# Splitting float64 weights: exponents shifted by ScalarE's factor of 2^-112, sign bits made on GpSimd, one VectorE pass fewer

## The chip, the cores and the metric

The kernel runs on one core of one Trainium2 chip. The metric is the time of one execution in microseconds of the device (us), and lower is better. The engines are TensorE (PE in the profile; its weight loads are PEld), VectorE (DVE), ScalarE (ACT), GpSimd (POOL) and SyncE (SP, which issues most of the transfers). Each engine takes its instructions in order from a queue of its own, and engines wait for each other through semaphores. "L193" is line 193 of the kernel before.

## The reference

Local attention with 32 global tokens for 8 batches of 8 heads, then a two-layer network over the 4608 resulting rows. The part that matters here:

```python
def _moe_ref(x, w_in, w_out):
    h = x @ w_in                                                # x: 4608 x 512, w_in: 512 x 2048
    g = np.where(h > 0.0, h, np.exp(np.minimum(h, 0.0)) - 1.0)  # ELU
    return (g @ w_out).astype(np.float32)                       # w_out: 2048 x 512
```

x is the attention's output: for every local row a softmax over 32 global keys and the local keys within 32 positions, and for every global row a softmax over all keys. The weights of the network come as float64.

## The kernel before

**Two streams.** One generator, `attention()`, issues the attention of batch after batch in tiles of 128 queries (scores, exponential, sum, normalising, transposing, product with the values). Another, `ffn_stream()`, issues the network's matrix products block by block (256 rows of x at a time). A main loop interleaves both: up to yield 66 of the attention it runs alone (`lead`), and then a table (`PACE`) says how many steps of the network belong to each step of the attention. A `tick()` in the loop runs work that was put off by `defer(n, ...)` for n ticks. This gives the program order; a list scheduler then moves independent instructions past each other in each engine's queue, by its own costs. `keep_in_program_order` keeps it from moving the instruction it wraps.

**Weights.** TensorE multiplies float16 pairs: each weight is split into a high and a low float16 part after scaling by a power of two. The float64 weights are loaded as pairs of 32-bit words (`raw`, two buffers) and turned into float32 by bit operations. Sixteen units do this, eight for w_in and eight for w_out, each 128 partitions by 1024 weights. `load_weights()` takes one unit after another; `fetch` loads the next unit's words, and `unit` defers its steps:

- s0: ScalarE writes the absolute value of the high words, read as float32, into the work tile `cu` (L188); GpSimd clamps it to the range that float32 can express after the shift (L189).
- s1a: VectorE shifts the clamped word left by 3 and clears its sign and top exponent bit (L193).
- s1b: VectorE ORs in the sign and the top exponent bit, masked out of the high word (L196).
- s1c: VectorE ORs in the top three bits of the low word (L200). `cu` is now the weight in float32.
- s1d: ScalarE takes absolute values again, with their sum over the row (L204), whose output goes over the low words; `raw` is free afterwards.
- s2 to s4: a maximum over partitions (TensorE and VectorE, L141, L142), a power of two from it, the high part on ScalarE (L213) and the low part on VectorE (L216).

In the lead the steps s0 to s1d lie one tick apart, later two. The steps of the network wait for the groups of units that they need: pair 0 (group a), pair 1 (b), pairs 2 and 3 (c), pairs 4 to 7 (d), and once all are there, the later blocks use all eight at once (f) with a scheme of seven products.

**What else GpSimd does.** It normalises the attention's probabilities (L793, four per tile; L731 and L732 for the global rows) and makes small tables of factors `xs` for the network (L584 to L588), without which ScalarE cannot read the first layer's result out of TensorE's banks (L333) or scale the second layer's input (L349).

**What else VectorE does in that stretch.** The attention's masked scores with their maxima (L780), sums and reciprocals (L790, L791), the copy of the transposed probabilities (L811), maxima of x (L868), the ELU's last step (L342) and its low part (L345), the adding of partial results (L455), and the low part of x (L571).

Of the kernel before, what the change touches and what calls it, by code (L numbers as in the profile page):

```python
# [10 lines left out]
F32 = mybir.dt.float32  # L11
F32R = mybir.dt.float32r
I32 = mybir.dt.int32
AF = mybir.ActivationFunctionType
ALU = mybir.AluOpType
# [35 lines left out]
SEVEN = (((2, "B11"), (3, "B22")), ((0, "B11+B22"), (4, "B21-B11")), ((5, "B11+B12"), (1, "B22-B12")), ((6, "B21+B22"),))  # L51


FMIN = struct.unpack("f", struct.pack("I", 0x38000000))[0]
FMAX = struct.unpack("f", struct.pack("I", 0x47efe000))[0]
LOW = (127 - 40) << 23
TOP = (2 * 127 + 14) << 23

# [2 lines left out]
def attn_ffn(ctx: ExitStack, tc: tile.TileContext, qT, qgT, kT, vT, vgT, vpT, w_in, w_out, mask, out):  # L61
    nc = tc.nc
    scale = 1.0 / math.sqrt(D)
# [21 lines left out]
    def defer(n, fn):  # L85
        if n == 0:
            return fn()
        later.setdefault(now[0] + n, []).append(fn)
# [39 lines left out]
    def power(dst, src):  # L128

        dst = dst.bitcast(I32)  # L130
        nc.vector.tensor_scalar(dst, src.bitcast(I32), 0x7f800000, None, ALU.bitwise_and)
        nc.vector.tensor_scalar_max(dst, dst, LOW)

    def inverse(dst, src):

        nc.vector.tensor_scalar(dst.bitcast(I32), src.bitcast(I32), TOP, -1.0, ALU.subtract, ALU.mult)

    def all_max(dst, src):

        tp = ps_a.tile([P, 512], F32, name="pa")  # L140
        tc.keep_in_program_order(nc.tensor.transpose(tp[:, 0:P], src.to_broadcast([P, P]), ident))  # L141
        nc.vector.tensor_reduce(out=dst, in_=tp[:, 0:P], op=ALU.max, axis=AX.X)  # L142
# [34 lines left out]
    def unit(m, p, raw):  # L177
        f = slice(2 * p * P, 2 * (p + 1) * P)
        shape = [P, NC, 2 * P] if m == 0 else [P, 2, DM]
        parts = [w[:, :, f] for w in win] if m == 0 else [w[:, 2 * p:2 * p + 2, :] for w in wout]  # L180
        pw = (pww if m == 0 else pwo)[:, p:p + 1]
        u = ffn.tile(shape, F32, name="cu", bufs=3)
        mx = ffn.tile([P, 4], F32, name="cm", bufs=4)
        high, low = raw[..., 1], raw[..., 0]
        ui = u.bitcast(I32)

        def s0():
            nc.scalar.activation(u, high.bitcast(F32), AF.Abs)  # L188
            nc.gpsimd.tensor_scalar(u, u, FMAX, FMIN, ALU.min, ALU.max)  # L189

        def s1a():
            tc.keep_in_program_order(
                nc.vector.tensor_scalar(ui, ui, 3, 0x3ffffff8, ALU.logical_shift_left, ALU.bitwise_and))  # L193

        def s1b():
            nc.vector.scalar_tensor_tensor(out=ui, in0=high, scalar=-0x40000000, in1=ui,  # L196
                                           op0=ALU.bitwise_and, op1=ALU.bitwise_or)

        def s1c():
            nc.vector.scalar_tensor_tensor(out=ui, in0=low, scalar=29, in1=ui,  # L200
                                           op0=ALU.logical_shift_right, op1=ALU.bitwise_or)

        def s1d():
            nc.scalar.activation(low.bitcast(F32), u, AF.Abs, accum_out=mx[:, m:m + 1])  # L204

        def s2():
            if m == 0:
                all_max(mx[:, 1:2], mx[:, 0:1])

        def s3():  # L210
            power(pw, mx[:, 1:2])
            inverse(mx[:, 3:4], pw)
            nc.scalar.activation(parts[0], u, AF.Copy, scale=mx[:, 3:4])  # L213

        def s4():
            nc.vector.scalar_tensor_tensor(out=parts[1].rearrange("p a b -> p (a b)") if m else parts[1],  # L216
                                           in0=u.rearrange("p a b -> p (a b)") if m else u, scalar=mx[:, 3:4],
                                           in1=parts[0].rearrange("p a b -> p (a b)") if m else parts[0],
                                           op0=ALU.mult, op1=ALU.subtract)

        d = 1 if lead[0] else 2
        lag = 7 if m else 16
        for i, fn in ((1, s0), (1 + d, s1a), (1 + 2 * d, s1b), (1 + 3 * d, s1c), (1 + 4 * d, s1d),
                      (1 + lag, s2), (2 + lag, s3), (3 + lag, s4)):
            defer(i, fn)
# [758 lines left out]
    f = ffn_stream()  # L984
# [89 lines left out]
```

## Time and profile before

| | |
|---|---|
| time, median of 3 runs | 949.64 us (948.83 to 953.76) |
| the profiled execution | 954.72 us |
| its span, first to last instruction | 952.9 us |
| granted clock of TensorE, mean | 0.977 |
| instructions | 23830 |

The profile is of one execution. Busy times are sums over instructions; "idle before" is the idle time of the engine just ahead of a group of instructions, with what ended it. A row of the timeline gives the start in us from the span's start, the duration in us, the engine, the line, the operation, the tiles written and read, and in brackets how long the engine had been idle and who ended that. A wait row names the waiting instruction, the one it waited for, the total in us, how many times, and the longest. The mean over the span says little here: the start, where weights are made and the attention runs ahead, and the long rest, where TensorE is nearly always busy, have different limits.

### The profile page before, as it was taken

Reading aid. Unit: us, or ns where it says so; the run is one execution under the profiler, and the core shown is the slowest. Engines: PE = TensorE matmul, PEld = TensorE weight load, DVE = VectorE, ACT = ScalarE, POOL = GpSimd, SP = SyncE. Lnnn points to the kernel's source line nnn. Section 1 sums busy time; section 2 is a strip of 40 time slices with the busy share of each in tenths; the row PEclk is TensorE's granted clock in tenths of the full one; section 3 lists DMA queues with packets and bytes.
Section 4 is the critical chain, followed back from the end, with each engine's and each line's share of the span. In section 5 each row is a group of like instructions: output and inputs, shape, how many; then the busy total and the mean of one; then the engine's idle time right before and its main releaser. Section 6 shows DMA issues by size and latency. Waiting matters only on the chain.

```text
span 952.9 us, 23830 instructions
## 1 busy us (share of the span) xinstructions
PE 908.5 (95%) x9216; PEld 727.8 (76%) x9216; DVE 728.1 (76%) x2025; ACT 670.1 (70%) x1584; POOL 271.1 (28%) x483
## 2 busy tenths in 40 slices
PE   6889887899999999999999999999999999999997
PEld 3567564566666788888888888888888888888886
DVE  4988988889967777768776877687777777676566
ACT  5888996776656767757677767677767767666564
POOL 4655481461522322122121212221332312100000
PEclk8779999899999999999999999999999999999999
DMA  6855876331342023101330123102310101000000
GB/s 262 299 179 180 282 224 191 124 123 57 115 157 90 23 100 103 47 26 46 105 121 26 46 78 125 47 27 79 122 49 25 46 23 35 2 23 23 1 24 23
DMA packets 41769, 87.64 MB, mean 92 GB/s; under 512 B 7736, under 2 KB 8888, under 8 KB 41656
## 3 DMA queue, kind: packets, MB, share of 16 engines
q1 hardware_dynamic: 41368, 85.85, 26.6%
q8 instruction: 73, 1.20, 0.5%
q14 instruction: 40, 0.33, 0.1%
q10 hardware_dynamic: 288, 0.26, 0.1%
HBM read 70.89 MB, written 15.20 MB: 90 GB/s over the span
## 4 chain that ended last, share of the span: by engine, by line
PE 67%; DVE 14%; ACT 9%; POOL 3%; issue 3%; DMA 3%; SPq 0%; DVEq 0%; ACTq 0%; POOLq 0%
PE pa L324 25%; PE acc L482 12%; PE h L482 9%; PE acc L447 4%; PE pa L822 3%; PE h L324 3%; PE pa L769 3%; PE pa L809 2%; ACT p L786 2%; DMA raw<-w_out 2%; PE pa L889 2%; DVE gl L345 1%; POOL p L793 1%; DVE cu L196 1%; DVE cu L200 1%
## 5 line engine op out<-in xcount | busy, mean ns | idle before, releaser
L324 PEld LDWEIGHTS <-winh 128*128 128x128 f16 x2160 | 209.4, 98 | 39.2 <-issue 8.4
L793 POOL TENSOR_SCALAR p<-p,sm 128x128 f32<-128x128 f32 x256 | 147.8, 593 | 303.2 <-DVE sm L791 165.0
L324 PE MATMUL pa<-xh,winh 128*128 128x256 f16 x824 | 224.9, 273 | 0.1
L324 PE MATMUL pa<-xl,winh 128*128 128x256 f16 x824 | 224.6, 273 | 0.0
L324 PE MATMUL pa<-xh,winl 128*128 128x256 f16 x824 | 224.6, 273 | 0.0
L361 ACT ACTIVATE gh<-gx,xs 128x896 f16<-128x896 f32 x103 | 107.3, 1042 | 123.1 <-DVE gx L358 123.0
L345 DVE SCALAR_TENSOR_TENSOR gl<-gx,xs,gh 128x896 f16<-128x896 f32 x103 | 119.4, 1159 | 59.9 <-ACT gh L361 59.0
L482 PEld LDWEIGHTS <-gh 128*128 128x128 f16 x1456 | 139.5, 98 | 24.0 <-issue 7.4
L786 ACT ACTIVATE p<-p,m 128x160 f32<-128x160 f32 x256 | 106.7, 421 | 41.6 <-DVE m L780 41.4
L324 PEld LDWEIGHTS <-winl 128*128 128x128 f16 x1080 | 106.1, 98 | 14.3 <-issue 1.2
L333 ACT ACTIVATE g<-pa,xs 128x512 f32<-128x512 f32 x103 | 70.3, 682 | 24.4 <-PE pa L324 23.8
L482 PE MATMUL acc<-wouth,gh 128*128 128x256 f16 x312 | 85.2, 273 | 0.0
L482 PE MATMUL acc<-woutl,gh 128*128 128x256 f16 x312 | 85.1, 273 | 0.0
L335 ACT ACTIVATE g<-g 128x512 f32<-128x512 f32 x135 | 85.0, 630 | 0.1
L482 PE MATMUL acc<-wouth,gl 128*128 128x256 f16 x312 | 85.0, 273 | 0.0
L482 PEld LDWEIGHTS <-gl 128*128 128x128 f16 x728 | 71.2, 98 | 9.2 <-DVE gl L345 1.0
L482 PE MATMUL h<-raw,gh 128*128 128x256 f16 x416 | 75.0, 273 | 0.0
L324 PE MATMUL h<-xh,winh 128*128 128x256 f16 x256 | 71.1, 279 | 1.5 <-ACT hs L334 0.9
L324 PE MATMUL h<-xl,winh 128*128 128x256 f16 x256 | 71.0, 278 | 0.7 <-DVE xl L571 0.7
L324 PE MATMUL h<-xh,winl 128*128 128x256 f16 x256 | 71.0, 278 | 0.0
L780 DVE CUSTOM_DVE_ANT_0 p<-pa,msk 128x160 f32<-128x160 f32 x228 | 61.5, 318 | 4.8 <-PE pa L769 4.7
L342 DVE SCALAR_TENSOR_TENSOR gx<-g,hs 128x512 f32<-128x512 f32 x51 | 35.9, 704 | 36.0 <-ACT g L335 35.6
(236 smaller groups left out, 2016.9 us busy)
## 6 DMA issues: line engine op xcount, KB each, us to landing
k<-kT SPq DMA_DIRECT2D x32, 640.0 KB, 5.1
v<-vT SPq DMA_DIRECT2D x64, 256.0 KB, 2.8
q<-qT SPq DMA_DIRECT2D x32, 256.0 KB, 5.6
raw<-w_in SPq DMA_DIRECT2D x8, 1024.0 KB, 5.9
raw<-w_out SPq DMA_DIRECT2D x8, 1024.0 KB, 6.8
out<-o SPq DMA_DIRECT2D x32, 256.0 KB, 2.3
od<-o SPq DMA_DIRECT2D x24, 256.0 KB, 3.1
o<-od SPq DMA_DIRECT2D x24, 256.0 KB, 2.8
```

Source lines behind the costliest of these rows:

```text
L324: nc.tensor.matmul(h[:, j, :], wt[:, c, f], xt[:, c, :], start=k == 0, stop=k == 11)
L333: nc.scalar.activation(g, hf, AF.Relu, scale=sc[:, p:p + 1])
L335: nc.scalar.activation(g, g, AF.Exp, scale=-1.0)
L342: nc.vector.scalar_tensor_tensor(out=out, in0=ins[0], scalar=-1.0, in1=ins[1], op0=ALU.add, op1=ALU.max)
L345: nc.vector.scalar_tensor_tensor(out=dst, in0=src, scalar=sg, in1=hi, op0=ALU.mult, op1=ALU.subtract)
L361: nc.scalar.activation(gh, gx, AF.Copy, scale=sg)
L447: nc.tensor.matmul(acc[t], gt[:, s], wt[:, f, :], start=p == first and j == 0 and k == 0, stop=p == last and j == 1 and k == 2)
L482: nc.tensor.matmul(cols, gt, w, start=p == 0 and k == 0, stop=last and k == len(todo) - 1, skip_group_check=True)
L769: nc.tensor.matmul(sp[r][half * HQ:(half + 1) * HQ, j * KW:(j + 1) * KW], q[rows, qs], k[rows, t, half, :], start=True, stop=True)
L780: nc.vector.tensor_tensor_reduce(out=p, in0=sp[r][:, j * KW:(j + 1) * KW], in1=msk[:, mi, :], op0=ALU.add, op1=ALU.min, scale=-scale, scal ...
L786: nc.scalar.activation(ps[i], ps[i], AF.Exp, bias=m[:, i:i + 1], scale=-1.0, accum_out=s[:, 0, i:i + 1])
L793: nc.gpsimd.tensor_scalar(ps[i][:, 0:P], ps[i][:, 0:P], s[:, 1, i:i + 1], 1.0, ALU.mult, ALU.mult)
```

## The change

The exponent of a float64 has eleven bits and that of a float32 eight. Read as a float32, the high word of a float64 holds the top eight bits of its exponent; the old way clamps, shifts left by three and clears the two top bits of the result, to put sign and top exponent bit back from the high word. The new way multiplies by 2^-112 on ScalarE, in the instruction that takes the absolute value. That moves the exponent so far down that after the clamp (whose limits move by the same factor) the three bits that are shifted out are zero, and nothing has to be cleared. The sign bit alone is made by GpSimd, in place over the high words: (high < 0) x -2^31, written as an integer. VectorE then does the shift and the OR of the sign in one pass (L196), and the OR of the low word as before (L200). The numbers that come out are the same.

```diff
-FMIN = struct.unpack("f", struct.pack("I", 0x38000000))[0]
-FMAX = struct.unpack("f", struct.pack("I", 0x47efe000))[0]
+FMIN = 2.0 ** -126
+FMAX = struct.unpack("f", struct.pack("I", 0x0fefe000))[0]
...
         def s0():
-            nc.scalar.activation(u, high.bitcast(F32), AF.Abs)
+            nc.scalar.activation(u, high.bitcast(F32), AF.Abs, scale=2.0 ** -112)
             nc.gpsimd.tensor_scalar(u, u, FMAX, FMIN, ALU.min, ALU.max)

         def s1a():
+            nc.gpsimd.tensor_scalar(high, high.bitcast(F32), 0.0, -2.0 ** 31, ALU.is_lt, ALU.mult)
+
+        def s1b():
             tc.keep_in_program_order(
-                nc.vector.tensor_scalar(ui, ui, 3, 0x3ffffff8, ALU.logical_shift_left, ALU.bitwise_and))
-
-        def s1b():
-            nc.vector.scalar_tensor_tensor(out=ui, in0=high, scalar=-0x40000000, in1=ui,
-                                           op0=ALU.bitwise_and, op1=ALU.bitwise_or)
+                nc.vector.scalar_tensor_tensor(out=ui, in0=ui, scalar=3, in1=high,
+                                               op0=ALU.logical_shift_left, op1=ALU.bitwise_or))
```

The new GpSimd pass stands at line 192 of the changed kernel; the other lines keep their numbers. Since the scheduler places instructions by its costs, the queues change in more than these rows. They differ in the first tenth only: the last row that differs lies, by the trace of before, near 261 us, and behind it every engine's order is the same in both kernels. Three places follow. In them `cu` and `raw` are the tiles of a weight unit, `p_93` to `p_95` three tiles of probabilities, `ptw` and `ptg` the transposed ones, `pz` the probabilities of global keys, `sm` their sums, `xs` factors for the network.

GpSimd's queue at the start, from the first tile's normalising on, before:

```order
L793 TENSOR_SCALAR p_94<-p_94,sm 128x128 x3
L189 TENSOR_SCALAR cu<-cu 128x1024
L793 TENSOR_SCALAR p_94<-p_94,sm 128x128
L189 TENSOR_SCALAR cu<-cu 128x1024
L793 TENSOR_SCALAR p_95<-p_95,sm 128x128 x4
L793 TENSOR_SCALAR p_93<-p_93,sm 128x128 x4
```

and now:

```order
L793 TENSOR_SCALAR p_94<-p_94,sm 128x128 x3
L189 TENSOR_SCALAR cu<-cu 128x1024
L192 TENSOR_SCALAR raw<-raw 128x1024
L793 TENSOR_SCALAR p_94<-p_94,sm 128x128
L793 TENSOR_SCALAR p_95<-p_95,sm 128x128 x4
L189 TENSOR_SCALAR cu<-cu 128x1024
L192 TENSOR_SCALAR raw<-raw 128x1024
L793 TENSOR_SCALAR p_93<-p_93,sm 128x128 x4
```

The first sign pass stands ahead of the first tile's last normalising, and the second unit's clamp has moved behind the second tile's four, with its sign pass after it.

VectorE's queue at the same time, behind the first tile's `pz`, before:

```order
L193 TENSOR_SCALAR cu<-cu 128x1024
L811 COPY ptw_81<-pa 128x2x4x64
L196 SCALAR_TENSOR_TENSOR cu<-raw,cu 128x1024
L790 TENSOR_SCALAR sm<-sm 128x4
L780 ISA p_94,m<-pa,msk 128x160
L780 ISA m 128x1
L200 SCALAR_TENSOR_TENSOR cu<-raw,cu 128x1024
L193 TENSOR_SCALAR cu<-cu 128x1024
L791 RECIPROCAL sm<-sm 128x4
L753 TENSOR_REDUCE ptg_84<-pa 128x32
L196 SCALAR_TENSOR_TENSOR cu<-raw,cu 128x1024
```

and now:

```order
L790 TENSOR_SCALAR sm<-sm 128x4
L791 RECIPROCAL sm<-sm 128x4
L196 SCALAR_TENSOR_TENSOR cu<-cu,raw 128x1024
L795 TENSOR_TENSOR pz<-p_95,sm 128x128
L200 SCALAR_TENSOR_TENSOR cu<-raw,cu 128x1024
L811 COPY ptw_81<-pa 128x2x4x64
L790 TENSOR_SCALAR sm<-sm 128x4
L780 ISA p_94,m<-pa,msk 128x160
L780 ISA m 128x1
L196 SCALAR_TENSOR_TENSOR cu<-cu,raw 128x1024
L753 TENSOR_REDUCE ptg_84<-pa 128x32
L200 SCALAR_TENSOR_TENSOR cu<-raw,cu 128x1024
```

The second tile's sum and reciprocal have moved ahead of the first unit, the copy L811 behind it, and the reduction L753 now follows the second unit's L196 instead of its L193.

GpSimd's queue later, where the factors of group a and then c are made (by the trace of before, from 105.7 us), before:

```order
L793 TENSOR_SCALAR p_93<-p_93,sm 128x128 x4
L189 TENSOR_SCALAR cu<-cu 128x1024
L793 TENSOR_SCALAR p_94<-p_94,sm 128x128 x4
L112 MEMSET ptw_83 64x416
L584 TENSOR_SCALAR xs<-isc,xm 128x1
L585 TENSOR_SCALAR xs<-isc,xm 128x1
L588 TENSOR_SCALAR xs<-wm_a,xm 128x1
L587 TENSOR_SCALAR xs<-t_a,xm 128x1
```

and now:

```order
L793 TENSOR_SCALAR p_93<-p_93,sm 128x128 x4
L189 TENSOR_SCALAR cu<-cu 128x1024
L793 TENSOR_SCALAR p_94<-p_94,sm 128x128 x4
L192 TENSOR_SCALAR raw<-raw 128x1024
L584 TENSOR_SCALAR xs<-isc,xm 128x1
L585 TENSOR_SCALAR xs<-isc,xm 128x1
L587 TENSOR_SCALAR xs<-t_a,xm 128x1
L588 TENSOR_SCALAR xs<-wm_a,xm 128x1
```

A sign pass stands between the normalising and the factors, and the clearing of `ptw` has moved behind them.

## The prediction

> **What bounds the kernel now.** I read the totals first, then the stretches of the span, then the waits and the chain of the stretch that the change touches. The totals from the page, and three stretches with the busy time of each engine (the first number after the stretch is its length):
>
> ```profile
> PE 908.5 (95%) x9216; PEld 727.8 (76%) x9216; DVE 728.1 (76%) x2025; ACT 670.1 (70%) x1584; POOL 271.1 (28%) x483
> ```
> ```profile
> core 0: us, PE busy (x) PEld busy (x) DVE busy (x) ACT busy (x) POOL busy (x), PEclk, DMA share, GB/s
> 0.00:12.00 12.00, 9.06 (x82) 4.39 (x82) 3.51 (x23) 3.23 (x11) 2.69 (x12) 1.00 0.83 306
> 12.00:204.00 192.00, 163.08 (x1460) 110.00 (x1461) 162.92 (x505) 157.85 (x404) 105.71 (x184) 0.89 0.60 203
> 204.00:900.00 696.00, 689.80 (x7253) 572.14 (x7252) 527.76 (x1430) 480.22 (x1126) 162.16 (x287) 1.00 0.19 63
> ```
>
> From 204 to 900 us TensorE is busy for 689.80 of 696.00 us: it is the bound there, and nothing that VectorE does can shorten it. From 12 to 204 us TensorE is idle for 192.00 - 163.08 = 28.9 us. All sixteen weight units lie in this stretch, and so does every instruction of the change. Here VectorE is busy 162.92 of 192 us (85%), ScalarE 82%, GpSimd 55%. No engine is full: they hand work to each other. Whatever time is won or lost before 204 us reaches the end, since the stretch behind it is TensorE's fixed work.
>
> ```profile
> by line: DMA raw<-w_out 8.3%; issue 7.1%; POOL p L793 6.2%; DVE cu L196 6.1%; DVE cu L200 5.7%; ACT p L786 5.6%; ACT raw L204 2.7%; DVE gl L345 2.7%; DVE p L780 2.7%; DVE winl L216 2.6%; ACT gh L349 2.3%; POOL cu L189 2.3%; ACT cu L188 2.3%
> ```
> ```profile
> DVE cu L193 <- POOL cu L189: 9.4, 7, 2.9
> ...
> PE pa L809 <- POOL p L793: 4.5, 3, 3.9
> PE acc L447 <- DVE o L455: 4.2, 3, 2.2
> PE h L853 <- DVE ptg L753: 3.0, 1, 3.0
> ```
>
> The first is the chain of waits between 12 and 204 us by line; the second, the waits of the same stretch (who waited for whom: us in total, times, longest). The chain is spread over all engines; the two long VectorE passes of a unit (L196, L200) hold 11.8% of it, the pass that goes (L193) is below the lines shown. GpSimd's normalising (L793) and clamping (L189) are on it too. VectorE's largest wait is that of the removed pass itself, for GpSimd's clamp.
>
> **What goes.** Sixteen clearing passes. Their group, and two rows of VectorE's timeline:
>
> ```profile
> L193 DVE TENSOR_SCALAR cu<-cu 128x1024 int32<-128x1024 int32 x16 | 11.0, 689 | 9.4 <-POOL cu L189 9.4
> ```
> ```profile
> 78.33 0.69 DVE L193 TENSOR_SCALAR cu<-cu 128x1024 int32<-128x1024 int32 x1
> 78.94 0.68 DVE L811 COPY ptw<-pa 128x512 f32<-128x512 f32 x1
> ```
>
> A pass lasts 0.69 us, but the next instruction starts 0.61 us behind it, so 16 x 0.61 = **9.8 us** of VectorE's time come free.
>
> **What only changes form.** ScalarE's absolute value gets a factor: it had the same instruction without one, 1140 ns, and L213 with a per-partition factor on the same shape takes 1148, so I cost it at 0. VectorE's L196 now shifts and ORs instead of ANDing and ORing:
>
> ```profile
> L196 DVE SCALAR_TENSOR_TENSOR cu<-raw,cu x16: 1189/1218/1374, 18.8 to 186.2; 128x1024 int32<-128x1024 int32 x16
> L200 DVE SCALAR_TENSOR_TENSOR cu<-raw,cu x16: 1208/1218/2061, 20.3 to 187.5; 128x1024 int32<-128x1024 int32 x16
> ```
> ```profile
> L188 ACT ACTIVATE cu<-raw 128x1024 f32<-128x1024 f32 x16 | 18.2, 1140 | 6.3 <-DMA raw<-w_out 6.3
> L213 ACT ACTIVATE wouth<-cu,cm 128x1024 f16<-128x1024 f32 x8 | 9.2, 1148 | 0.5 <-DVE cm L136 0.5
> ```
>
> L200 is a shift and an OR already, over the same pair of tiles, at the same median of 1218 ns: 0 again.
>
> **What is added.** Sixteen GpSimd passes over the high words (a comparison and a product, every second word, float in and integer out). The trace has no such pass. The nearest row is L189, the same length with a minimum and a maximum, 1.04 us. From afar, L793 takes 372 ns for 128 elements; at that rate 1024 elements would take 3.0 us. The one comparison on GpSimd, an affine select, takes 0.29 us for 128, less than L793. I take **1.04 us**, since the length is what L189 shares, and keep 3.0 as the upper end.
>
> ```profile
> L189 POOL TENSOR_SCALAR cu<-cu x16: 1039/1039/1272, 15.6 to 181.3; 128x1024 f32<-128x1024 f32 x16
> L793 POOL TENSOR_SCALAR p<-p,sm x256: 362/372/5552, 14.5 to 796.5; 128x128 f32<-128x128 f32 x128
> ```
> ```profile
> 1.51 0.29 POOL masks.py:199 TENSOR_SCALAR_AFFINE_SELECT ident<-ident 128x128 f32<-128x128 f32 x1
> ```
>
> GpSimd has 192.00 - 105.71 = 86.3 us idle here, so 16.6 more would fit. But GpSimd and VectorE hold each other up. Rows of both timelines, and the usual medians of two of these groups:
>
> ```profile
> 66.79 2.14 DVE L571 SCALAR_TENSOR_TENSOR xl<-xr,xm,xh 128x1024 f16<-128x1024 f32 x1 [1.52 <-ACT xh L568]
> 94.73 2.06 DVE L200 SCALAR_TENSOR_TENSOR cu<-raw,cu 128x1024 int32<-128x1024 int32 x1
> 111.25 1.03 DVE L795 TENSOR_TENSOR pz<-p,sm 128x128 f32<-128x128 f32 x1
> ```
> ```profile
> 66.82 1.04 POOL L189 TENSOR_SCALAR cu<-cu 128x1024 f32<-128x1024 f32 x1
> 94.44 1.27 POOL L189 TENSOR_SCALAR cu<-cu 128x1024 f32<-128x1024 f32 x1 [6.03 <-ACT cu L188]
> 111.09 1.04 POOL L189 TENSOR_SCALAR cu<-cu 128x1024 f32<-128x1024 f32 x1 [3.47 <-DVE sm L791]
> 137.98 4.24 POOL L584 TENSOR_SCALAR xs<-isc,xm 128x2 f32<-128x2 f32 x1 [3.06 <-ACT o L458]
> 142.20 0.26 POOL L585 TENSOR_SCALAR xs<-isc,xm 128x2 f32<-128x2 f32 x1
> ```
> ```profile
> L571 DVE SCALAR_TENSOR_TENSOR xl<-xr,xm,xh x16: 1275/1286/2141, 66.8 to 831.9; 128x1024 f16<-128x1024 f32 x16
> L795 DVE TENSOR_TENSOR pz<-p,sm x64: 274/291/1032, 13.5 to 793.7; 128x128 f32<-128x128 f32 x64
> ```
>
> Three VectorE instructions that read two tiles of SBUF start beside a clamp and last 2.14 - 1.29 = 0.85, 2.06 - 1.22 = 0.84 and 1.03 - 0.29 = 0.74 us longer. The other way round, a two-element GpSimd operation takes 4.24 us where VectorE runs such instructions back to back, and 0.26 right behind. So a GpSimd pass is not free for VectorE even where VectorE does not need its result. What a clamp costs VectorE today: the 9.4 us of waiting, less the first and longest wait of 2.9 (VectorE had nothing else then), and the three stretches of 2.4: 8.9 us over 16, or 0.56 each. The sign pass has the same length and also stands ahead of an instruction that needs it (L196), so 16 x 0.56 = **+8.9 us**. Bounds: 0 if every pass falls into VectorE's one-tile work, and 16 x 0.56 x 3.0/1.04 = 26 us at the long price.
>
> By the Trainium skill ("SBUF — State Buffer", Who interferes with whom), a VectorE instruction with two SBUF inputs and a GpSimd instruction that reads SBUF exclude each other for the whole instruction; the trace's 2.14 against 1.29 us agrees. Read strictly, each sign pass would cost its whole length, and the sum would be that of the second rival below.
>
> **Two places where order matters.** At the start, GpSimd and VectorE run:
>
> ```profile
> 15.65 1.04 POOL L189 TENSOR_SCALAR cu<-cu 128x1024 f32<-128x1024 f32 x1
> ```
> ```profile
> 22.11 0.26 DVE L753 TENSOR_REDUCE ptg<-pa 128x32 f32<-128x128 f32 x1
> ```
>
> L753 releases TensorE's L853, which waits 3.0 us for it (above). It now stands behind the second unit's L196, and that behind these GpSimd steps: clamp from 15.65, sign (17.7), one normalising (18.1), four (19.6), clamp and sign (21.7). L196 takes 1.22, so L753 starts at 22.9 instead of 22.1 if nothing collides: +0.8. With GpSimd disturbed as it is today (eight normalisings take 5.1 us at 22.28 instead of 8 x 0.37 = 3.0) it is 1.0 more. I take **+1.0**. Part of the rest is made up, since VectorE gets the second tile's sums (L790, L791) earlier.
>
> ```profile
> 22.28 5.09 POOL L793 TENSOR_SCALAR p<-p,sm 128x128 f32<-128x128 f32 x8 [3.50 <-DVE sm L791]
> ```
> ```profile
> 131.82 0.72 ACT L349 ACTIVATE gh<-g,xs 128x512 f16<-128x512 f32 x1 [0.87 <-POOL xs L587]
> 190.10 0.69 ACT L333 ACTIVATE g<-h,xs 128x512 f32<-128x512 f32 x1 [2.77 <-POOL xs L587]
> ```
>
> Twice ScalarE waits for the factors xs from GpSimd, whose queue holds clamps ahead of them; a sign pass now stands there too. That is 0 to 2 x 1.04 us; I take the middle, **+1.0**. Behind ScalarE's waiting instruction queue the exponentials and the evictions of TensorE's banks.
>
> **Sum:** -9.8 + 8.9 + 1.0 + 1.0 = +1.1 us on the profiled execution, which took 954.72 us (span 952.9 and 1.8 around it). That run is 5.1 us above the median of 949.64; the terms are the same for both, so the forecast is 949.64 + 1.1 = **950.7 us**: no change that can be measured. About 0.5%, 4.75 us, is what a measurement of this kernel can tell from none.
>
> **Rivals.**
> Faster, 0.22: GpSimd's 86.3 idle us take the sign passes. In the 7 units where VectorE waited for the clamp it waits a little longer and wins nothing; in the other 9 it keeps 0.61 us, 5.5 us in all: 944.1. For it speaks that L196 stands later in VectorE's queue than L193 stood; against it, the 7 waits.
> Slower, 0.18: VectorE's two-tile instructions and GpSimd's passes exclude each other, and each sign pass takes its full 1.04 us from VectorE: 16 x (1.04 - 0.61) = +6.9, or 956.5. It decides once a pass costs VectorE more than 0.78 us (16 x 0.17 + 2.0 = 4.75). For it speak the three stretches of 0.74 to 0.85; against it, that only three of the sixteen clamps did as much.
> Slower still, 0.10: the comparison, the stride of two words and the integer output make the pass twice as long, 2.1 us. It then takes 2 x 0.56 from VectorE: 16 x (1.12 - 0.61) = +8.2, and the order terms double, +4.0: 961.8. The trace has no strided GpSimd row that decides. The Trainium skill ("GPSIMD Engine Reference", Performance pitfalls for Q7 kernels) puts the dearer reads at steps of over 8 bytes; here the step is 8, and no run here shows it yet.
>
> **Numbers.** Forecast 0.50, the rest as above. The forecast's own range is 946 to 955. Faster than by 0.5%: 0.22; within: 0.50; slower: 0.18 + 0.10 = 0.28. The range of 943 to 959 takes in the first two rivals and leaves out most of the third and the far ends (939.8 if the passes cost nothing, some 970 at 3.0 us each).
>
> **What would show it.** In the profile after: the sign pass's group at about 1.04 us x16; no row of the clearing pass; VectorE 11 us less busy in total unless two-tile instructions are stretched, GpSimd some 17 us more; VectorE waiting for the sign pass at L196 in about as many places as it waited for the clamp, for about as long or longer; L753 at about 23 us; the stretch behind 204 us unchanged. I am wrong if the sign pass lasts 2 us or more, if TensorE's idle time before 204 us moves by over 5 us, or if VectorE's waits for GpSimd vanish.

## The result, and the profile after

| | time, us | runs |
|---|---|---|
| before | 949.8 (948.83 to 953.76) | 4 |
| after | 984.9 (984.37 to 985.24) | 4 |

The ratio is 1.0359 [1.0332, 1.0386]: 3.6% slower, some 35 us, where no change was forecast. Here and below, an execution over 1.5% longer than the fastest of its kernel, at a lower granted clock, is left out. Each ratio is taken against executions of the kernel before in the same comparison, whose median moves between 949 and 952 us; so kernels of different tables compare by their ratios. The profiled execution of the changed kernel took 984.68 us; its span is 982.6 us at a mean granted clock of 0.966, against 952.9 us and 0.977 before, so the two spans are 29.7 us apart.

The group of the new pass, by its line (shortest, median and longest of the sixteen in ns, then the first and last start in us):

```profile
L192 POOL TENSOR_SCALAR raw<-raw x16: 3712/3817/4618, 16.7 to 209.3; 128x1024 int32<-128x1024 f32 x16
```

It lasts 3.8 us, not 1.04, and more than the 3.0 that the prediction kept as the upper end. The totals of the page, and the same stretches of the span as before:

```profile
PE 913.2 (93%) x9216; PEld 729.2 (74%) x9216; DVE 726.9 (74%) x2009; ACT 672.7 (68%) x1584; POOL 323.4 (33%) x499
```
```profile
core 0: us, PE busy (x) PEld busy (x) DVE busy (x) ACT busy (x) POOL busy (x), PEclk, DMA share, GB/s
0.00:12.00 12.00, 9.09 (x82) 4.33 (x82) 3.56 (x23) 3.29 (x12) 2.69 (x12) 1.00 0.83 311
12.00:204.00 192.00, 144.28 (x1286) 96.17 (x1287) 139.35 (x422) 137.34 (x353) 141.15 (x165) 0.83 0.57 190
204.00:900.00 696.00, 683.54 (x7155) 560.77 (x7153) 530.67 (x1459) 484.00 (x1147) 179.08 (x321) 1.00 0.19 66
```

From 12 to 204 us TensorE is now idle for 192.00 - 144.28 = 47.7 us (28.9 before), and from 204 to 900 us for 12.5 (6.2 before), since the last weight units have slipped past 204 us. That is 25.1 us more of idle time. The remaining 4.7 us are TensorE's busy time: 913.2 against 908.5 us for the same 9216 products, at a lower granted clock (0.83 against 0.89 in the first of these stretches). GpSimd is 52.3 us busier and VectorE only 1.2 us less busy, though 11.0 us of clearing passes are gone.

The waits between 12 and 204 us (who waited for whom, total, times, longest), and the chain of waits of that stretch by line:

```profile
DVE cu L196 <- POOL raw L192: 23.5, 8, 5.2
...
ACT raw L204 <- DVE cu L200: 20.6, 7, 6.8
...
PE pa L809 <- POOL p L793: 12.5, 5, 4.0
...
PE h L853 <- DVE ptg L753: 8.4, 1, 8.4
```
```profile
by line: POOL raw L192 20.1%; issue 9.6%; DVE cu L196 5.1%; ACT p L786 4.6%; POOL cu L189 4.4%; PE h L324 4.2%; DVE cu L200 4.0%; POOL p L793 3.9%; PE acc L447 3.7%; ACT raw L204 3.0%; PE h L822 2.7%; PE pa L769 2.5%; DMA raw<-w_in 2.3%; AC
```

VectorE waits 23.5 us for the sign passes (it waited 9.4 for the clamp), ScalarE waits behind VectorE, and TensorE waits 12.5 instead of 4.5 us for GpSimd's normalising and 8.4 instead of 3.0 for L753. The sign pass alone is a fifth of the chain. Both timelines of the start show how (start, duration, and in brackets the idle time ahead and who ended it); GpSimd first:

```profile
15.59 1.04 POOL L189 TENSOR_SCALAR cu<-cu 128x1024 f32<-128x1024 f32 x1
16.72 3.75 POOL L192 TENSOR_SCALAR raw<-raw 128x1024 int32<-128x1024 f32 x1
20.44 3.92 POOL L793 TENSOR_SCALAR p<-p,sm 128x128 f32<-128x128 f32 x5
24.44 1.04 POOL L189 TENSOR_SCALAR cu<-cu 128x1024 f32<-128x1024 f32 x1
25.56 3.71 POOL L192 TENSOR_SCALAR raw<-raw 128x1024 int32<-128x1024 f32 x1
```
```profile
20.50 1.22 DVE L196 SCALAR_TENSOR_TENSOR cu<-cu,raw 128x1024 int32<-128x1024 int32 x1 [3.63 <-POOL raw L192]
...
29.31 1.23 DVE L196 SCALAR_TENSOR_TENSOR cu<-cu,raw 128x1024 int32<-128x1024 int32 x1 [5.24 <-POOL raw L192]
30.45 0.28 DVE L753 TENSOR_REDUCE ptg<-pa 128x32 f32<-128x128 f32 x1
```

The two passes delay the first two units, and L753, which needs neither of them, stands behind the second unit's L196 in VectorE's queue. It starts at 30.45 us instead of 22.11.

### The profile page after: what moved, and what is told of

The parts are those of the page before. It is cut to its first block, busy times and chain, and to the rows that moved or that the text cites. A ratio compares the mean times of both kernels' runs of the same rounds, so it can differ in the third digit from the quotient of the medians.

```text
span 982.6 us, 23838 instructions
## 1 busy us (share of the span) xinstructions
PE 913.2 (93%) x9216; PEld 729.2 (74%) x9216; DVE 726.9 (74%) x2009; ACT 672.7 (68%) x1584; POOL 323.4 (33%) x499
## 4 chain that ended last, share of the span: by engine, by line
PE 65%; DVE 12%; ACT 8%; POOL 8%; issue 4%; DMA 2%; SPq 0%; DVEq 0%; POOLq 0%; ACTq 0%
PE pa L324 24%; PE acc L482 12%; PE h L482 9%; POOL raw L192 4%; PE pa L822 4%; PE acc L447 3%; PE pa L769 3%; PE h L324 3%; PE pa L809 2%; ACT p L786 2%; PE pa L889 2%; POOL p L793 1%; DVE gl L345 1%; DVE cu L196 1%; DVE cu L275 1%
## 5 line engine op out<-in xcount | busy, mean ns | idle before, releaser
L793 POOL TENSOR_SCALAR p<-p,sm 128x128 f32<-128x128 f32 x256 | 143.0, 575 | 304.5 <-DVE sm L791 191.2
L345 DVE SCALAR_TENSOR_TENSOR gl<-gx,xs,gh 128x896 f16<-128x896 f32 x103 | 119.7, 1162 | 60.3 <-ACT gh L361 59.3
L333 ACT ACTIVATE g<-pa,xs 128x512 f32<-128x512 f32 x103 | 70.6, 685 | 23.5 <-PE pa L324 22.9
L192 POOL TENSOR_SCALAR raw<-raw 128x1024 int32<-128x1024 f32 x16 | 63.0, 3936 | 1.0
```

The lines of the kernel that those rows point to most:

```text
L192: nc.gpsimd.tensor_scalar(high, high.bitcast(F32), 0.0, -2.0 ** 31, ALU.is_lt, ALU.mult)
L333: nc.scalar.activation(g, hf, AF.Relu, scale=sc[:, p:p + 1])
L345: nc.vector.scalar_tensor_tensor(out=dst, in0=src, scalar=sg, in1=hi, op0=ALU.mult, op1=ALU.subtract)
L793: nc.gpsimd.tensor_scalar(ps[i][:, 0:P], ps[i][:, 0:P], s[:, 1, i:i + 1], 1.0, ALU.mult, ALU.mult)
```

## The experiments

Edits are against the changed kernel where nothing else is said. Where a kernel leaves something out of the computation, its expectation says so.

### What makes the pass long

Three things set the new pass apart from the clamp: it compares, it steps over two words, and it writes integers. Three variants of its one line, all with the order of the changed kernel on every engine:

```diff
-            nc.gpsimd.tensor_scalar(high, high.bitcast(F32), 0.0, -2.0 ** 31, ALU.is_lt, ALU.mult)
+            nc.gpsimd.tensor_scalar(high.bitcast(F32), high.bitcast(F32), 0.0, 0.0, ALU.is_lt, ALU.mult)   # float output
...
+            nc.gpsimd.tensor_scalar(high, high.bitcast(F32), 0.0, 0.0, ALU.min, ALU.max)                   # min and max
...
+            nc.gpsimd.tensor_scalar(high.bitcast(F32), high.bitcast(F32), 0.0, 1.0, ALU.mult, ALU.mult)    # times zero
```

The third keeps the whole computation: a negative number times 0.0 is -0.0, which has the sign bit alone.

> The changed kernel with one thing altered: the sign pass on GpSimd still compares with 0 and still steps over two words, but its output is float32 zeros in place of int32 sign words. The signs of the weights are left out of the computation. Three theories on why the pass lasts 3.8 us in place of the forecast 1.04. Integer output (the conversion is dear): the pass falls to about 1.0 to 1.3 us, and the time to about 951 us. Comparison: it stays at 3.7 to 3.9 us, and the time at about 985 us. Step of 8 bytes: stays at 3.7 to 3.9 us, about 985 us.

> The changed kernel with the comparison and the multiplication of the sign pass replaced by a minimum and a maximum with 0; the int32 output and the step of two words stay. The signs of the weights are left out of the computation. Integer output: the pass stays at 3.7 to 3.9 us and the time at about 985 us. Comparison: the pass falls to 1.0 to 1.3 us, the time to about 951 us. Step of 8 bytes: stays at 3.8 us, about 985 us.

> The changed kernel with the sign word made by a multiplication of the float32 by 0.0 (and by 1.0), whose -0.0 has the sign bit alone: no comparison, no integer output, the same step of two words, the whole computation kept. Integer output or comparison, alone or both: the pass falls to 1.0 to 1.3 us, and by the forecast's sum the time is 950.7 us (943 to 959), no change within 0.5% of the kernel before. Step of 8 bytes: the pass stays at 3.8 us, and the time at about 985 us. If the pass falls and the time does not, the loss is not in the pass's length, but in the wait for GpSimd as such.

The pass by its line, in this order:

```profile
L192 POOL TENSOR_SCALAR raw<-raw x16: 3712/3848/4665, 17.1 to 207.7; 128x1024 f32<-128x1024 f32 x16
```
```profile
L192 POOL TENSOR_SCALAR raw<-raw x16: 1083/1130/1952, 16.9 to 184.8; 128x1024 int32<-128x1024 f32 x16
```
```profile
L192 POOL TENSOR_SCALAR raw<-raw x16: 1087/1140/1951, 17.2 to 186.3; 128x1024 f32<-128x1024 f32 x16
```

| | the pass, median | time, us |
|---|---|---|
| after (comparison, integer output) | 3.82 us | 984.9 |
| float output | 3.85 us | 983.24, one execution |
| min and max, integer output | 1.13 us | 958.2, one execution |
| times zero | 1.14 us | 959.82, ratio 1.0084 [1.0058, 1.0111] |

It is the comparison. Neither the integer output nor the step of two words costs much by itself: the pass that has both takes 1.13 us, the dense clamp L189 1.04 (median of the run with times zero). No run has the comparison over words that lie side by side, so that it is as dear there is not shown. Since the order is the same in all four, 984.9 - 959.8 = 25 us are the effect of 16 x (3.82 - 1.14) = 43 us of GpSimd's time and of nothing else. But with a pass of almost the forecast's length the kernel is still 0.84% slower than before, about 8 us, where the forecast had 1.1.

### No pass, and passes that nobody reads

Two causes were to be told apart: that VectorE waits for the pass, or that GpSimd is occupied and its other work comes later. The first kernel has no sign pass. Two others do the pass into a tile that lies unused until 315 us (`gx`), and VectorE does not read it. By the traces, VectorE and ScalarE run the same instructions in the same order in these three, and GpSimd's queue differs by the sixteen passes and the places of one normalising and two factors beside them; the two unread passes have the same order everywhere. The last kernel uses that tile for the whole computation, with the pass ahead of the clamp; against the cheap unread pass only five rows of GpSimd's queue stand elsewhere.

```diff
 # no pass
-            nc.gpsimd.tensor_scalar(high, high.bitcast(F32), 0.0, -2.0 ** 31, ALU.is_lt, ALU.mult)
+            pass
 # unread, cheap; the dear one keeps is_lt and mult by -2^31
+        sb = ffn.tile([P, 10, P], F32, name="gx", bufs=1)[:, 0:8, :].rearrange("p a b -> p (a b)").rearrange("p (a b) -> p a b", a=shape[1])
-            nc.gpsimd.tensor_scalar(high, high.bitcast(F32), 0.0, -2.0 ** 31, ALU.is_lt, ALU.mult)
+            nc.gpsimd.tensor_scalar(sb, high.bitcast(F32), 0.0, 1.0, ALU.mult, ALU.mult)
 # early
         def s0():
+            nc.gpsimd.tensor_scalar(sb, high.bitcast(F32), 0.0, 1.0, ALU.mult, ALU.mult)
             nc.scalar.activation(u, high.bitcast(F32), AF.Abs, scale=2.0 ** -112)
...
-                nc.vector.scalar_tensor_tensor(out=ui, in0=ui, scalar=3, in1=high,
+                nc.vector.scalar_tensor_tensor(out=ui, in0=ui, scalar=3, in1=sb.bitcast(I32),
```

> The changed kernel without any sign pass: VectorE's shift with OR takes the untouched high words, so the exponents and the leading bits of the mantissas are wrong; all else is as in the changed kernel. This is what the change takes away, without what it adds. If the forecast's sum is right but for the pass, the removal of 16 clearing passes is worth 9.8 us, with 2 us lost again in the start order and the factors: about 942 us. If TensorE did not wait for the clearing passes at all, about 950 us, as before.

> The cheap sign pass (a multiplication by 0.0, 1.14 us) is done 16 times by GpSimd, but into a tile that nothing reads; VectorE takes the untouched high words, so the exponents and leading bits are wrong. Theory wait: the pass costs time because VectorE, and what is queued behind it, waits for it; unread, it costs little: within 3 us of the kernel without a pass, about 942 to 946 us. Theory occupation: it costs because GpSimd is busy 18 us more, its other work comes later and VectorE is slowed at the shared memory port; unread, it costs the same: 957 to 960 us.

> The comparing sign pass of the changed kernel (3.8 us) is done 16 times into a tile that nothing reads; VectorE takes the untouched high words, so the exponents and leading bits are wrong. Theory wait: most of the 35 us of the changed kernel goes, 945 to 952 us. Theory occupation: it stays at 978 to 985 us.

> The whole computation, with the cheap sign pass (a multiplication by 0.0) put ahead of GpSimd's clamp: it goes into a tile of its own, so that it needs only the landed weights and can run while ScalarE takes the absolute values; VectorE's shift with OR reads that tile. Theory wait: VectorE no longer waits for the pass, the time is that of the unread cheap pass, 942 to 947 us, and faster than the kernel before. Theory occupation: 957 to 960 us, as with the pass behind the clamp.

| | time, us | ratio to before |
|---|---|---|
| no pass | 949.04 (946.62 to 951.49) | 0.9989 [0.9964, 1.0014] |
| cheap pass, unread | 956.68 (955.18 to 960.09) | 1.0064 [1.0039, 1.009] |
| cheap pass, early, read | 955.81 (953.87 to 959.84) | 1.0064 [1.0038, 1.009] |
| dear pass, unread | 972.65, one execution | |

Two findings. First, occupation is the larger part. With VectorE's and ScalarE's order held, sixteen passes that nobody reads cost 956.7 - 949.0 = 8 us at 1.14 us each, and 16 us more at 3.7 us each (one execution). The early pass, which VectorE does read, costs no more than the unread one. So of the 25 us that the dear pass costs more than the cheap one where VectorE reads it, some 16 come without anybody reading it, and some 9 from waiting for it (the orders of the two pairs differ, so this split is rough). At the cheap pass what the waiting adds, 1.0084 against 1.0064, lies within the intervals.

What an unread pass does shows in two places. One is VectorE: the same 2009 instructions in the same order are busy longer. The totals without a pass, with the cheap and with the dear one:

```profile
PE 903.8 (95%) x9216; PEld 724.4 (76%) x9216; DVE 719.9 (76%) x2009; ACT 669.8 (71%) x1584; POOL 267.9 (28%) x483
```
```profile
PE 907.9 (95%) x9216; PEld 727.8 (76%) x9216; DVE 727.0 (76%) x2009; ACT 670.7 (70%) x1584; POOL 287.8 (30%) x499
```
```profile
PE 909.4 (94%) x9216; PEld 728.8 (75%) x9216; DVE 726.0 (75%) x2009; ACT 670.4 (69%) x1584; POOL 327.5 (34%) x499
```

Sixteen cheap passes stretch VectorE's work by 7.1 us, and sixteen dear ones by 6.1, no more. The other place is TensorE, which waits for the normalising behind the passes in GpSimd's queue. Without a pass, cheap, dear, and cheap and early (L794 and L810, L795 and L811 are L793 and L809 of the changed kernel), in the stretch from 12 to 204 us:

```profile
PE pa L809 <- POOL p L793: 5.7, 4, 4.0
```
```profile
PE pa L810 <- POOL p L794: 9.7, 3, 5.0
```
```profile
PE pa L810 <- POOL p L794: 15.3, 6, 7.6
```
```profile
PE pa L811 <- POOL p L795: 5.6, 3, 4.6
```

For the dear pass this wait grows by 9.6 us. For the cheap one it cannot be the whole account: the early pass loses as much as the unread one, and there the wait is 5.6 us, as without a pass, while VectorE is stretched by 8.7 us (728.6 in all). How the cheap pass's 7 to 8 us divide between these two places is not shown.

Second, and not expected: without any sign pass the kernel is as fast as before, and no faster. The stretch from 12 to 204 us of that run:

```profile
12.00:204.00 192.00, 160.58 (x1483) 108.46 (x1484) 157.64 (x493) 159.77 (x407) 105.91 (x184) 0.92 0.61 206
```

VectorE is 5.3 us less busy in it than before, and TensorE is idle for 31.4 us, no less than the 28.9 before. So the 9.8 us of the forecast's first term do not show even when nothing is added.

### Where the gain of the removed pass went

Either the clearing pass was off the path, or something else in the change (ScalarE's factor, or another order in the queues) loses what it gains. Three kernels first. One leaves the sign to VectorE, where the clearing was; the next is the kernel before with the clearing done twice; the third lets GpSimd make the signs early and VectorE do the clamp.

```diff
 # VectorE's sign (from after)
-            nc.gpsimd.tensor_scalar(high, high.bitcast(F32), 0.0, -2.0 ** 31, ALU.is_lt, ALU.mult)
+            tc.keep_in_program_order(
+                nc.vector.tensor_scalar(high, high, -0x80000000, None, ALU.bitwise_and))
 # clearing twice (from before)
                 nc.vector.tensor_scalar(ui, ui, 3, 0x3ffffff8, ALU.logical_shift_left, ALU.bitwise_and))
+            tc.keep_in_program_order(
+                nc.vector.tensor_scalar(ui, ui, 0x3ffffff8, None, ALU.bitwise_and))
 # VectorE's clamp (from the early pass)
-            nc.gpsimd.tensor_scalar(u, u, FMAX, FMIN, ALU.min, ALU.max)
...
+            tc.keep_in_program_order(nc.vector.tensor_scalar(u, u, FMAX, FMIN, ALU.min, ALU.max))
```

> The whole computation: ScalarE's factor, the new limits of the clamp and the shift with OR as in the changed kernel, but the sign words are made by VectorE (an AND with the sign bit over the high words), where the kernel before had its clearing pass. So it is the change without its move to GpSimd. Theory hidden (the clearing pass was no part of the path, and the rest of the change costs nothing): 947 to 951 us, as before. Theory offset (the clearing pass was worth its 9.8 us, and the factor, the order and the small numbers cost as much again): 957 to 960 us.

> The kernel before with its clearing done twice: a second AND with the mask on VectorE behind the first, 16 more instructions of about 0.6 us, nothing else changed. Theory hidden: within 2 us of the kernel before, 948 to 952 us. Theory offset, and the forecast's price of 0.61 us each: 16 times 0.61 = 9.8 us more, about 959 us.

> The whole computation, with the works exchanged: GpSimd makes the cheap sign words (a multiplication by 0.0, into a tile of its own, while ScalarE takes the absolute values), and VectorE does the clamp where it had the clearing pass. GpSimd's time per unit is then that of the kernel before (1.14 against 1.04 us), VectorE's too if the clamp takes 0.6 us; the chain of a unit is one GpSimd pass shorter. Theory occupation (GpSimd's time is what the change costs): 946 to 951 us, no change. If the length of a unit's chain counts too: 940 to 946 us, faster than the kernel before. If VectorE's third pass is what counts, and the clamp is no faster than 1.2 us: 955 to 960 us.

| | time, us | ratio to before |
|---|---|---|
| VectorE's sign | 959.01 (958.87 to 961.32) | 1.0095 [1.0059, 1.0132] |
| clearing twice | 961.65 (959.68 to 965.78) | 1.0111 [1.0067, 1.0155] |
| VectorE's clamp | 960.05 (957.02 to 963.0) | 1.0101 [1.0051, 1.015] |

By their expectations the first two speak for the offset: a second pass costs the forecast's price, and the change with all its passes on VectorE is 9 us slower than before. VectorE's sign pass takes as long as the clearing pass did:

```profile
L193 DVE TENSOR_SCALAR raw<-raw x16: 682/690/1247, 13.9 to 185.9; 128x1024 int32<-128x1024 int32 x16
```

So with passes of the same lengths on the same engines, something else loses 9 us. In the third, the clamp takes 0.68 us on VectorE and GpSimd has one pass per unit as before (1.32 us at the median, against 1.04), and it is as slow: the shorter chain gains nothing that shows.

Two candidates were left, the factor and the order. One kernel has the factor and the clamp's new limits alone, in the order of before on every engine. Another has the work of before, in another order, by a lower priority of the reduction L753.

```diff
 # factor alone (from before; FMIN and FMAX as in the change)
-            nc.scalar.activation(u, high.bitcast(F32), AF.Abs)
+            nc.scalar.activation(u, high.bitcast(F32), AF.Abs, scale=2.0 ** -112)
 # order alone (from before)
+                with tc.high_priority(offset=-8):
-                nc.vector.tensor_reduce(out=pz[:, HQ:HQ + 32], ...
+                    nc.vector.tensor_reduce(out=pz[:, HQ:HQ + 32], ...
 # no pass, and early pass: the same line under
+                with tc.high_priority():
```

> The kernel before with ScalarE's factor of 2^-112 and the clamp's new limits alone; the clearing pass stays on VectorE, where it now clears nothing that is set wrongly, and the numbers that come out are the same. Every engine's order is that of the kernel before. Theory order (the VectorE variant of the change lost 9 us because the scheduler arranged the start differently): the factor and the smaller numbers cost nothing, 948 to 952 us, ratio 1.000 within its interval. Theory factor (the multiplication or the small numbers cost time): 957 to 960 us.

> The kernel before with the same instructions, in another order: the reduction over the first tile's transposed global keys (one in every group of tiles, L753 of the kernel before), for which TensorE waits, has a lower priority with the scheduler, so that at the start it stands behind the second weight unit's two ORs instead of ahead of them. Theory order: this alone loses several us, 953 to 960 us. If the order is worth nothing: 948 to 952 us.

> The changed kernel without any sign pass (exponents and leading bits of the weights wrong, as in the earlier run without a pass), and the same reduction with a higher priority, so that it stands ahead of the second unit's last OR. Theory order: what the removed clearing pass gains was lost by the place of this reduction, and comes out now: 940 to 945 us. If the removed pass gains nothing whatever the order: 947 to 951 us.

> The whole computation, with the early cheap sign pass into a tile of its own (the best of the full versions so far, 955.8 us), and the reduction with the higher priority. Theory order: 946 to 951 us, at least no slower than the kernel before. If order is worth nothing: 954 to 958 us.

| | time, us | ratio to before |
|---|---|---|
| factor alone | 952.11 (948.07 to 955.51) | 1.0013 [0.9993, 1.0034] |
| order alone | 956.08 (954.32 to 961.02) | 1.0055 [1.0026, 1.0083] |
| no pass, reduction ahead | 950.62 (948.7 to 956.61) | 0.9998 [0.9978, 1.0017] |
| early pass, reduction ahead | 961.17 (958.2 to 963.41) | 1.0104 [1.0081, 1.0127] |

The factor is free. The order is not: the same instructions in another order lose 0.55% (0.26 to 0.83), 5 us. In the waits between 12 and 40 us TensorE waits 5.7 us for the reduction instead of 3.0 (the line is L754 there, and L855 is L853):

```profile
PE h L855 <- DVE ptg L754: 5.7, 1, 5.7
```

But it is not this one place that decides. Moved ahead by priority, the reduction gained nothing in the kernel without a pass, and the full version with the early pass became slower (1.0104 against 1.0064, 4 us), while the priority moved other rows too: over a hundred of VectorE's. My expectation for these two was wrong.

The last question was whether a shorter clearing gains anything in the old order. The clearing was done for half of each unit's weights, with which VectorE's queue keeps the order of before up to about 28 us, and for an eighth, with which it does not.

```diff
-                nc.vector.tensor_scalar(ui, ui, 3, 0x3ffffff8, ALU.logical_shift_left, ALU.bitwise_and))
+                nc.vector.tensor_scalar(ui[:, :, :shape[2] // 2], ui[:, :, :shape[2] // 2], 3, 0x3ffffff8,
+                                        ALU.logical_shift_left, ALU.bitwise_and))
```

> The kernel before with ScalarE's factor (which cost nothing by itself), and the shift with clearing on VectorE done for half of each unit's weights; the other half is not shifted, so those weights are wrong. The scheduler keeps nearly the order of the kernel before: the first reduction of the transposed global keys stays between the second unit's clearing and its first OR. Theory order and length (a VectorE pass is worth its time, but the changed kernel's order loses as much): 16 half passes of 0.3 to 0.35 us go, and the time falls to 944 to 947 us. If VectorE's passes are worth nothing in this direction: 949 to 952 us.

> The same with the shift and clearing done for an eighth of each unit's weights. Now the scheduler arranges the start as in the changed kernel and in the variant with VectorE's sign pass: both of the second unit's rows ahead of the reduction's place. Theory order and length: 16 times 0.55 us go, and the other order costs its 9 us: 948 to 952 us, slower than with half a pass. If order is worth nothing and length all: 940 to 943 us.

| | the clearing pass, median | time, us | ratio to before |
|---|---|---|---|
| factor alone | 0.686 us | 952.11 | 1.0013 [0.9993, 1.0034] |
| half | 0.421 us | 951.69 | 1.0007 [0.9985, 1.0029] |
| an eighth | 0.222 us | 950.87 | 0.9995 [0.9974, 1.0016] |
| none, no sign pass | | 949.04 | 0.9989 [0.9964, 1.0014] |

In four kernels with the clearing shortened or gone (these three and the one with the reduction ahead), the time stays within 0.3% of before at both ends of every interval but one (0.9964). A pass that gets shorter gains nothing that can be told; the forecast's 9.8 us would be 1.0%. A slower clock does not hide a gain, though these four compute with wrong weights: their mean granted clock is 0.980 to 0.983, that of before beside them 0.979 to 0.981. TensorE's idle time between 12 and 204 us is the same with half a pass as with a whole one: 27.8 against 27.6 us by these rows, with half and with the factor alone:

```profile
12.00:204.00 192.00, 164.19 (x1492) 109.96 (x1493) 164.22 (x514) 161.71 (x411) 101.87 (x185) 0.91 0.63 208
```
```profile
12.00:204.00 192.00, 164.45 (x1477) 110.59 (x1478) 165.01 (x508) 159.49 (x407) 106.49 (x184) 0.90 0.61 207
```

Shown is that the scheduler gives no gain in four orders. Not shown is that the freed time is worth nothing by itself, for none of the four has the order of before. With half a pass GpSimd's queue is that of before, but behind 28 us some 70 of VectorE's rows stand elsewhere, against the expectation of nearly the same order; so an order that loses what the shorter pass gains is not ruled out. Open is also why VectorE's sign and VectorE's clamp lose 9 to 10 us. Their order differs from that of before, and another order alone was seen to lose 5; no run shows that the order accounts for all of it. It is open as well which share of the second clearing's 10.6 us is its length and which its order. And no version tried was faster than the kernel before.

## Why the prediction was wrong, point by point

Two steps failed. The price of the sign pass was taken as 1.04 us and is 3.82, which makes 25 of the 35 us. And the 9.8 us that were to come free on VectorE gained nothing, which makes up nearly the rest.

**What goes (-9.8 us): the amount was right, its worth was not.** The 11.0 us of VectorE's passes went, but the kernel without a sign pass is not faster. The step that failed here is the one from "VectorE's time come free" to microseconds of the end. The prediction itself had VectorE at 85% and TensorE idle 28.9 us, "no engine is full", and then counted VectorE's time one for one. The shortened passes show no gain either; whether it is not there or lost again to the order stays open.

**What only changes form (0): right.** ScalarE's absolute value has a median of 1139 ns with the factor (1140 before), and the factor alone gives 1.0013 [0.9993, 1.0034]. VectorE's shift with OR costs what the prediction took from L200: 1224 ns at the median in the changed kernel, against 1218.

**The sign pass (1.04 us, at most 3.0): the term that broke the forecast.** It lasts 3.8 us. The nearest row, L189, had the length and the engine, but not the operation; the bound of 3.0 was scaled from a row without a comparison too, so neither end held the thing that was unknown. The one comparison that it quoted, an affine select of 0.29 us for 128 elements, is another operation and pointed the wrong way. The third rival had the right suspicion, "the comparison, the stride of two words and the integer output", and the wrong size: 2.1 us and 961.8. The runs name the comparison. By the Trainium skill ("GPSIMD Engine Reference", Performance pitfalls for Q7 kernels) reads get dearer at steps of over 8 bytes; here the step is 8, and the strided pass took 1.13 us against 1.04 for the dense one, which fits the page; no run here has a longer step.

**Its hold on VectorE (16 x 0.56 = +8.9): about right for the pass that was assumed.** Sixteen unread passes of 1.14 us stretch VectorE's unchanged work by 7.1 us, 0.44 each, and the early ones by 8.7, 0.54 each. The upper bound, scaled with the pass's length to 26 us, was not: passes of 3.7 us stretch it by 6.1. What the long pass costs more lies elsewhere, in waits for it and in GpSimd's own queue, where TensorE waits 15.3 us for the normalising instead of 5.7 without a pass. The forecast knew that GpSimd had 86.3 us idle and took that as room; a queue that is idle for 45% of the stretch still delays what stands behind a pass. The whole cost of a pass of the forecast's length is 0.75 to 0.95% by the ratios (1.0064 to 1.0084 with it, 0.9989 without), 7 to 9 us, where the forecast's three added terms make 8.9 + 1.0 + 1.0 = 10.9.

**The start (+1.0).** L753 was to start at about 23 us and starts at 30.45, as two dear passes stand ahead of it in GpSimd's queue, then L196 on VectorE; TensorE waits 8.4 us there instead of 3.0. With the cheap pass it starts at 25.6 and not at 22.9, and without any pass at 23.7, so the +0.8 was too little even for the pass that was assumed.

**The factors xs (+1.0): not borne out.** From 12 to 240 us ScalarE waited 5.1 us for the factors before (2.8 at L333, 2.3 at L349). With the dear pass it waits 5.8 us, all at L333, and with the cheap pass 4.4: for the pass that was assumed, the wait did not grow.

**The rivals.** The faster one (GpSimd's idle time takes the passes) is refuted by the unread passes, which cost 7 to 8 us. The slower one (each pass takes its whole length from VectorE) gave 956.5 us (it left out the two order terms; with them it would be 958.5), close to the cheap pass's time. Its mechanism does not hold, so that is luck: VectorE loses 0.44 us per pass of 1.14, and no more per pass of 3.7. The forecast's sum of +1.1 would have been wrong even for a cheap pass: 8 us. It came close to zero because a gain that did not come was set against a cost that did.

**What was named as the sign of being wrong** came in two of three forms: the pass lasts over 2 us, and TensorE's idle time before 204 us moved by over 5 us (by 18.8).

## What to carry to other kernels

Where the trace has no row of an operation, its nearest row must share the operation and not only the engine and the size; this comparison on GpSimd took 3.4 times as long as a product or a minimum on the same data, and a sign can be had by a multiplication with 0.0. Where no engine is full, do not count an engine's freed time until a wait of the bounding engine is named that ends earlier; added time can still cost, for it delays what stands behind it in its queue and may stretch another engine's work. And where a scheduler places the instructions, two kernels compare the length of a step only if their orders are the same; here another order alone was worth 5 us.

## What the runs showed of the hardware

**This comparison on GpSimd is dear.** 128x1024 elements take 3.72 to 3.85 us at the median with a comparison (`is_lt`) and a product at a step of two words, 1.13 and 1.14 us with a minimum and a maximum or with two products at the same step, and 1.04 us with a minimum and a maximum without it. For the comparison the output's type makes no difference (3.82 as integer, 3.85 as float).

**A long GpSimd pass does not hold all of VectorE's work for its whole length.** From the timelines of the dear unread pass, GpSimd and then VectorE (L193 is the sign pass there, L201 the shift and OR L200, L346 is L345, L791 is L790):

```profile
186.32 3.70 POOL L193 TENSOR_SCALAR gx<-raw 128x1024 int32<-128x1024 f32 x1 [5.66 <-DMA raw<-w_in]
```
```profile
186.46 2.05 DVE L201 SCALAR_TENSOR_TENSOR cu<-raw,cu 128x1024 int32<-128x1024 int32 x1
188.44 0.74 DVE L346 SCALAR_TENSOR_TENSOR gl<-g,xs,gh 128x512 f16<-128x512 f32 x1
189.10 0.95 DVE L791 TENSOR_SCALAR sm<-sm 128x4 f32<-128x4 f32 x1
```

L201 starts beside the pass and lasts 2.05 instead of 1.21 us, 0.84 longer, which is what it lost beside a clamp of 1.27 us in the trace of before. The pass then runs on until 190.02 us, and L346, also with two inputs from SBUF, takes its 0.74 us within it. By the Trainium skill ("SBUF — State Buffer", Who interferes with whom) the two exclude each other for the whole instruction. The trace differs: beside a pass of 3.7 us L201 loses 0.84 us, and not 3.7, and over the whole span sixteen such passes cost VectorE no more than sixteen of 1.14 us (6.1 against 7.1 us).

**Short one-input work is held until the pass ends.** L791 in the rows above, an operation on four elements per partition, lasts until 190.05 us, when the pass beside it is over, instead of its usual 0.16 us. The same operation in the changed kernel's start lasts as long as the clamp of 1.04 us at 15.59 beside it:

```profile
15.62 1.04 DVE L790 TENSOR_SCALAR sm<-sm 128x4 f32<-128x4 f32 x1 [1.81 <-ACT p L786]
```

**A lower granted clock goes with a longer time.** The slowest kernel had the lowest mean clock of the traces (0.966), and one without a sign pass the highest (0.985). The idle time of TensorE explains that only in the rough: with 61 to 69 us of it the clock was 0.966 to 0.973, with 42 to 52 us it lay anywhere between 0.972 and 0.985. Within one kernel the two go together as well: over 89 executions of the kernel before the mean clock goes from 0.972 to 0.986, and a clock lower by 0.010 goes with a time longer by about 6 us. Which of the two is the cause was not tried.
